# Block 0's output products six steps late, and output weights combined from stored parts

## The chip, the cores and the metric

The kernel runs on one core of a Trainium2 chip. The core has five engines that matter here: TensorE (PE, the matmuls), VectorE (DVE), ScalarE (ACT), GpSimd (POOL) and SyncE (SP, which here only issues transfers). The metric is the device time of one execution in microseconds, as the median of several runs. The kernel before takes 1850.32 us (three runs, 1848.4 to 1851.07).

## The reference

Everything is float32, and the kernel reaches that accuracy by splitting both operands of the large products into a high and a low part.

```python
# attention with keys and values pooled by 8: q, k, v are (8, 8, 576, 64)
k_p, v_p = k.reshape(..., 72, 8, 64).mean(3), v.reshape(..., 72, 8, 64).mean(3)
x = softmax(q @ k_p.T / 8) @ v_p                # to (4608, 512)
# first FFN, d_ff = 2048
h = x @ w_in
g = s * maximum(h, 0)**2 + b
x = g @ w_out
# second FFN, d_ff = 1536
out = (sigmoid(x @ w_gate) * (x @ w_val)) @ w_out2
```

## The kernel before, in words

The 4608 tokens are nine blocks of 512. Attention is done in 18 units of 256 tokens, and the first FFN follows it block by block. Block 0 is computed plainly; blocks 1 to 8 form four pairs, whose output product g @ w_out is done by a scheme of the Strassen kind, with seven products of half-size operands for eight. Its left operands are sums and differences of quarters of w_out, `s1d[x][m]`, which are made once and kept in DRAM; m runs over eight (H1) because w_out's 16 tiles of 128 rows are taken as m and m + 8.

All weights arrive as 64-bit words. `convert` (line 78) makes float32 of a tile in four operations: line 85 on ACT, then lines 86, 87 and 88 on DVE. `split` (line 54) makes a high part on ACT (line 56) and a low part on DVE or POOL (line 57). A product is then three matmuls: high with low, high with high, low with high. `emit_h` (line 259) is one step of the first product, 12 matmuls of 128x512 for 128 of the 2048 columns (lines 269 to 271), followed by relu and square on ACT. `emit_x` (line 411) is the matching output product of block 0, 12 matmuls (lines 419 to 421); `mm_chunk` (line 357) is that of a pair: 6 matmuls for its first three groups of eight chunks and 12 for the last two (lines 370 to 372).

The work from block 0 to the last pair is a list of 176 slots: 16 of block 0, then 40 for each of four pairs. Each slot issues, in this order: the stores that the slot before left behind (`store_later`, line 149, on POOL's queue), the load of the input weights of three steps ahead (`load_wi`, line 129, on SP), a step of the first product, a part of the second FFN's weight preparation (`prep_w2`, line 228), a part of the output weights' combination (`prep_s`, line 178), the conversions of block 0's weights, the splitting of the operands of the output product, attention events for later units, and the output product of two slots before (LAG = 2).

In block 0 each weight tile is converted, split, used and stored (`w1d`, `s1d[0]`, `s1d[1]`, `s1d[3]`). The converted output weights stay in SBUF as `wf[m]`, in the pool of the `gs` tiles, until `prep_s` combines them in slots 14 to 29: six small operations on POOL for each m, then two splits into raw tiles and four stores. The sum `wsum` over all m serves the bias. The raw pool has three tiles of 512 KB and serves the loads of 64-bit weights as well; the pool for input weights has three tiles, the pool for output weights (`wr`) three, the pool for g three.

The order of instructions on PE and SP is the written one from slot 16 on; DVE, ACT and POOL, and all engines before slot 16, are ordered by a scheduler. SP issues in order, so a transfer that waits holds back those behind it.

After slot 175 the second FFN runs over the same pairs. Per m it makes seven products of half-size operands from `w7d[m]` (lines 882 to 884); its gated result goes through `emit_o` (line 929, matmuls in lines 938 to 940) in two phases, the second of which has the weights `wo2d[m]` loaded again. `fetch_w7` and `fetch_wo` are on SP. The operands of its first pair are made by `gen_x` (line 750) in the last pair of the first FFN.

Of the kernel before, what the change touches and what calls it, by code (L numbers as in the profile page):

```python
# [10 lines left out]
I32 = mybir.dt.int32  # L11
# [8 lines left out]
def pooled_attention_two_ffn(ctx, tc, q, k, v, v_left, w_in, w_out, s_in, b_in, w_gate, w_val, w_out2, out):  # L20
# [42 lines left out]
    s1d = [[dram.tile([128, 2, 256], F32, name=f"s1d{x}_{m}") for m in range(H1)] for x in range(7)]  # L63
# [56 lines left out]
    wi_raw, wi, wo_raw, wo, wf = {}, {}, {}, {}, {}  # L120
# [43 lines left out]
    def split_wo(i):  # L164

        if i < M1:
            m = steps[i][1]
            t = wr_tile().rearrange("p (two f) -> p two f", two=2)
            wf[m] = gs_tile()
            split(t[:, 0], t[:, 1], convert(wo_raw.pop(i), wf[m].bitcast(I32)), nc.gpsimd)  # L170
            wo[i] = t
            if m < H1:
                later.append((s1d[0][m], t[:, :, 0:256]))
            else:
                later.append((s1d[1][m - H1], t[:, :, 0:256]))
                later.append((s1d[3][m - H1], t[:, :, 256:512]))

    def prep_s(m, part):

        a, c = wf[m], wf[m + H1]  # L180
# [23 lines left out]
    def prep_bias():  # L204

        bb = cv_tile().bitcast(F32)[:, 0:128]
# [9 lines left out]

    prep = {}
# [41 lines left out]
    def emit_h(i):  # L259
# [12 lines left out]
        if j and m < H1:  # L272
# [138 lines left out]
    def emit_x(i):  # L411
# [10 lines left out]
        if i == M1 - 1:  # L422
            for d, a in enumerate(acc.pop(0)):
# [5 lines left out]
                nc.sync.dma_start(out=x2d[0][:, d, :], in_=eo)  # L429
# [64 lines left out]
    def pool_v_pe(b, what):  # L494

        n = NP if what == "v" else 2
        ps = ps_b.tile([128, n, D], F32, tag="b", name="vps")
# [17 lines left out]
    def place_left(b):  # L515
# [4 lines left out]
        lm = ls if b else at1.tile([128, 2, D], F32, tag="suml", name="lm")  # L520
# [123 lines left out]
    for b in range(1, B):  # L644
# [4 lines left out]
        at(max(p - 13, 0), load_kv, b, "v")  # L649
        at(max(p - 9, 1), pool_v, b, "v", nc.gpsimd)  # L650
# [28 lines left out]
    with tc.manual_schedule():  # L679
# [20 lines left out]
        load_wo(0)  # L700
# [17 lines left out]
        load_wo(1)  # L718
# [8 lines left out]
    if True:  # L727
        values(1, 0)
        values(1, 1)
        split_wo(0)  # L730
# [57 lines left out]

        chunks = [(None, i) for i in range(M1)] + [(p, x) for p in range(NB1) for x in range(5 * H1)]
        hidden, used = {}, []  # L790
        for slot, (p, x) in enumerate(chunks):
            if p is None:
                hidden[slot] = x
            elif x < 4 * H1:
                hidden[slot if p == 0 or x > 1 else slot - H1] = M1 * (1 + 2 * p) + x
            if p is None or x >= 3 * H1 or x % 2:
                used.append((slot + LAG, p, x))
        asked = M1
        light = [slot for slot, (p, x) in enumerate(chunks) if slot >= 2 * M1 + 2 and x < 4 * H1 and (x < 3 * H1 or x % 4 or p != 1)]
        parts = dict(zip(light, (divmod(i, 9) for i in range(9 * M2))))  # L800
        assert len(parts) == 9 * M2, len(parts)

        def mm(slot):
            p, x = chunks[slot]
            if p is None:
                emit_x(x)
            else:
                mm_chunk(p, x)

        pe_order = ExitStack()  # L810
        for slot, (p, x) in enumerate(chunks):
# [4 lines left out]
            store_later()  # L816
# [6 lines left out]
            if slot in parts:  # L823
                prep_w2(*parts[slot])
            if M1 - 2 <= slot < 2 * M1 - 2:
# [210 lines left out]
```

## Time and profile before

| | us |
|---|---|
| median of three runs | 1850.32 |
| profiled execution, device time | 1855.36 |
| profiled execution, span of the trace | 1853.6 |
| PE busy in the span | 1728.0 (93%) |
| DVE busy | 1085.4 (59%) |
| ACT busy | 747.6 (40%) |
| POOL busy | 522.5 (28%) |

The busy share is an average over stages that differ: attention with block 0 up to about 205 us, block 1 to about 306, the remaining pairs to about 1020, then the second FFN. A matmul's busy time overlaps with the next one's, so PE's share is not the share of its peak. Waits are put down to the event that came last.

### The profile page before, as it was taken

To read this page: it belongs to the slowest core of one execution; us is meant where nothing else is said; L and a number is where in the kernel's file an instruction comes from. 1 tells how busy PE (TensorE), PEld (TensorE's weight loads), DVE (VectorE), ACT (ScalarE), POOL (GpSimd) and SP (SyncE) were. 2 spreads that over 40 slices of the span, in tenths; PEclk is the share of its full clock that TensorE was granted. 3 is DMA by queue.
4 is the path that set the end of the run, shared out by engine and by line. 5 is a ranking of instruction groups with operands and counts; after the bars stand their busy time and mean duration, and the time that the engine had idled before them with its cause. 6 is when DMAs were issued, how large, how long until landed. Compare 5 with 4: busy or idle time off the path is not lost.

```text
span 1853.6 us, 22031 instructions
## 1 busy us (share of the span) xinstructions
PE 1728.0 (93%) x7848; PEld 1425.2 (77%) x7848; DVE 1085.4 (59%) x1636; ACT 747.6 (40%) x1331; POOL 522.5 (28%) x615
## 2 busy tenths in 40 slices
PE   4677899999999899989997999999999999999999
PEld 4556688877877777878785888788878887888887
DVE  7999675767675757665486445454445444544111
ACT  2555555646654555546563322222222222222111
POOL 5767961345640645324350000100010001000100
PEclk7788999999999999999998999999999999999999
DMA  7665796888977888878977555755665467555675
GB/s 260 213 210 198 274 332 226 276 298 294 360 247 262 304 306 300 280 248 285 313 266 258 206 203 211 257 188 187 223 249 190 181 221 253 194 180 201 236 238 178
DMA packets 138044, 454.44 MB, mean 245 GB/s; under 512 B 15696, under 2 KB 16720, under 8 KB 137936
## 3 DMA queue, kind: packets, MB, share of 16 engines
q1 hardware_dynamic: 107664, 363.90, 56.4%
q0 software_dynamic: 21056, 72.37, 11.0%
q10 hardware_dynamic: 9216, 16.78, 2.4%
q8 instruction: 62, 1.02, 0.2%
q14 instruction: 46, 0.38, 0.1%
HBM read 371.20 MB, written 81.79 MB: 244 GB/s over the span
## 4 chain that ended last, share of the span: by engine, by line
PE 44%; DMA 3%; POOL 1%; DVE 1%; issue 1%; ACT 0%; SPq 0%; POOLq 0%
PE pc L884 5%; PE pc L882 5%; PE pc L883 5%; PE acc L938 5%; PE acc L940 5%; PE acc L939 5%; PE pb L882 4%; PE pb L884 4%; PE pb L883 4%; DMA wo<-wo2d 2%; POOL raw L57 1%; DMA w<-w7d 1%; DMA g<-b21d 0%; DMA raw<-in 0%; DVE gs L296 0%
## 5 line engine op out<-in xcount | busy, mean ns | idle before, releaser
L888 DVE TENSOR_TENSOR wk<-pc,wk 128x512 f32<-128x512 f32 x192 | 132.4, 690 | 240.7 <-PE pc L884 240.6
L269 PE MATMUL hps<-xl,wi 128*128 128x512 f32 (+1 forms) x584 | 233.4, 400 | 10.9 <-ACT wi L56 7.7
L271 PE MATMUL hps<-xh,wi 128*128 128x512 f32 (+1 forms) x584 | 229.0, 393 | 0.4 <-POOL wi L57 0.4
L270 PE MATMUL hps<-xh,wi 128*128 128x512 f32 (+1 forms) x584 | 229.0, 392 | 0.0
L948 POOL DMA_DIRECT2D out<-eo x32 | 17.3, 543 | 691.0 <-ACT eo L946 685.4
L370 PE MATMUL acc<-gl,wr 128*128 128x512 f32 x448 | 182.5, 407 | 28.7 <-DVE gl L57 19.9
L372 PE MATMUL acc<-gh,wr 128*128 128x512 f32 x448 | 177.2, 396 | 0.0
L371 PE MATMUL acc<-gh,wr 128*128 128x512 f32 x448 | 177.2, 395 | 0.0
L899 ACT ACTIVATE g<-pb 128x512 f32<-128x512 f32 x60 | 35.9, 599 | 345.6 <-PE pb L884 345.6
L884 PE MATMUL pc<-xo,w 128*128 128x512 f32 x432 | 168.1, 389 | 0.0
L883 PE MATMUL pc<-xo,w 128*128 128x512 f32 x432 | 168.1, 389 | 0.0
L882 PE MATMUL pc<-xo,w 128*128 128x512 f32 x432 | 168.0, 389 | 0.0
L57 POOL TENSOR_TENSOR raw<-cv,raw 128x512 fp32r<-128x512 f32 (+1 forms) x72 | 99.3, 1385 | 225.5 <-ACT raw L56 222.3
L57 DVE TENSOR_TENSOR gl<-gs,gh 128x512 fp32r<-128x512 f32 x160 | 129.4, 822 | 34.6 <-ACT gh L56 32.2
L56 ACT ACTIVATE gh<-g 128x512 fp32r<-128x512 f32 x140 | 87.8, 627 | 150.4 <-DVE g L900 141.7
L56 ACT ACTIVATE gh<-gs 128x512 fp32r<-128x512 f32 x160 | 97.3, 627 | 109.3 <-DVE gs L296 106.2
L57 DVE TENSOR_TENSOR gl<-g,gh 128x512 fp32r<-128x512 f32 x140 | 113.6, 812 | 45.7 <-ACT gh L56 40.7
L269 PEld LDWEIGHTS hps<-xl,wi 128*128 128x128 f32 x584 | 112.9, 193 | 34.3 <-ACT wi L56 8.8
L882 PE MATMUL pb<-xo,w 128*128 128x512 f32 x336 | 131.4, 391 | 2.1 <-DMA w<-w7d 2.1
L883 PE MATMUL pb<-xo,w 128*128 128x512 f32 x336 | 131.5, 391 | 0.0
L884 PE MATMUL pb<-xo,w 128*128 128x512 f32 x336 | 131.4, 391 | 0.0
L271 PEld LDWEIGHTS hps<-xh,wi 128*128 128x128 f32 x584 | 111.6, 191 | 24.3 <-POOL wi L57 0.8
(145 smaller groups left out, 3843.2 us busy)
## 6 DMA issues: line engine op xcount, KB each, us to landing
w<-w7d SPq DMA_DIRECT2D x48, 1792.0 KB, 7.7
wi<-w1d SPq DMA_DIRECT2D x128, 512.0 KB, 4.6
wr<-s1d SPq DMA_DIRECT2D x224, 256.0 KB, 4.6
wo<-wo2d SPq DMA_DIRECT2D x108, 512.0 KB, 8.2
raw<-in SPq DMA_DIRECT2D x68, 512.0 KB, 4.8
w7d<-raw POOLq DMA_DIRECT2D x36, 512.0 KB, 5.6
w<-w7d SPq DMA_DIRECT2D x12, 1280.0 KB, 6.9
kv<-in SPq DMA_DIRECT2D x24, 512.0 KB, 6.1
```

Source lines behind the costliest of these rows:

```text
L56: nc.scalar.activation(out=hi, in_=src, func=ACTF.Copy)
L57: eng.tensor_tensor(out=lo, in0=src, in1=hi.bitcast(F32), op=ALU.subtract)
L269: nc.tensor.matmul(out=ps[:, f], lhsT=hi[:, kk], rhs=c[:, kk, f], start=kk == 0, stop=False)
L270: nc.tensor.matmul(out=ps[:, f], lhsT=hi[:, kk], rhs=a[:, kk, f], start=False, stop=False)
L271: nc.tensor.matmul(out=ps[:, f], lhsT=lo[:, kk], rhs=a[:, kk, f], start=False, stop=kk == KD - 1)
L370: nc.tensor.matmul(out=a, lhsT=w[:, 0, f], rhs=gl, start=begin, stop=False, skip_group_check=True)
L371: nc.tensor.matmul(out=a, lhsT=w[:, 0, f], rhs=gh, start=False, stop=False, skip_group_check=True)
L372: nc.tensor.matmul(out=a, lhsT=w[:, 1, f], rhs=gh, start=False, stop=end, skip_group_check=True)
L882: nc.tensor.matmul(out=ps, lhsT=w[:, 0, x, kk], rhs=r[:, 1, kk, :n], start=first and kk == 0, stop=False, skip_group_check=True)
L883: nc.tensor.matmul(out=ps, lhsT=w[:, 0, x, kk], rhs=r[:, 0, kk, :n], start=False, stop=False, skip_group_check=True)
L884: nc.tensor.matmul(out=ps, lhsT=w[:, 1, x, kk], rhs=r[:, 0, kk, :n], start=False, stop=kk == 1, skip_group_check=True)
L888: nc.vector.tensor_tensor(out=o, in0=ps, in1=b_, op=ALU.add)
```

## The change

Block 0's output products stand six steps behind its first products instead of two, and g of block 0 is kept in the `gs` pool. The conversion of w_out comes four slots later (slots 4 to 19), its loads in slots 2 to 17. Pair 0's first eight chunks are made two a slot (operands in slots 21 to 24, products in 22 to 25).

The output weights are combined in slots 16 to 31, from the stored parts: `s1d` gets an eighth part, every m reloads four quarters from DRAM into two raw tiles (a new line 186), DVE adds high and low part (line 191), POOL does four operations on 256 columns and one on 512 for `wsum`, whose halves are added once at the end.

Stores of slots 0 to 19 are issued on SP's queue instead of POOL's, and the four stores of block 0's result on ACT's instead of SP's. The values of batch 1 are pooled by matmuls on PE instead of additions on POOL. The second FFN's weights take eight parts for an m instead of nine (both first loads in one part), not in a pair's twelve-matmul chunks 24 to 31 except in the first pair, and two parts a slot in the last pair from its chunk 13 on. In the second FFN a fetch of the next pair's weights comes after the ninth product of the second phase instead of the fifth.

```diff
-    s1d = [[dram.tile([128, 2, 256], F32, name=f"s1d{x}_{m}") for m in range(H1)] for x in range(7)]
+    s1d = [[dram.tile([128, 2, 256], F32, name=f"s1d{x}_{m}") for m in range(H1)] for x in range(8)]
...
-    def store_later():
+    def store_later(early=False):
         while later:
             dst, t = later.pop(0)
-            nc.gpsimd.dma_start(out=dst, in_=t if t.dtype == F32 else t.bitcast(F32))
+            (nc.sync if early else nc.gpsimd).dma_start(out=dst, in_=t if t.dtype == F32 else t.bitcast(F32))
...
-            wf[m] = gs_tile()
-            split(t[:, 0], t[:, 1], convert(wo_raw.pop(i), wf[m].bitcast(I32)), nc.gpsimd)
+            split(t[:, 0], t[:, 1], convert(wo_raw.pop(i), cv_tile()), nc.gpsimd)
             wo[i] = t
-            if m < H1:
-                later.append((s1d[0][m], t[:, :, 0:256]))
-            else:
-                later.append((s1d[1][m - H1], t[:, :, 0:256]))
-                later.append((s1d[3][m - H1], t[:, :, 256:512]))
+            for h, x in enumerate((0, 7) if m < H1 else (1, 3)):
+                later.append((s1d[x][m % H1], t[:, :, 256 * h:256 * h + 256]))
...
         if part == 0:
+            prep["s"] = []
+            for xs in ((0, 7), (1, 3)):
+                t = raw_tile().bitcast(F32).rearrange("p (two f) -> p two f", two=2)
+                for h, x in zip((h0, h1), xs):
+                    nc.sync.dma_start(out=t[:, :, h], in_=s1d[x][m])
+                prep["s"].append(t)
+        else:
+            a, c = (t[:, 1] for t in prep["s"])
+            for t in prep["s"]:
+                nc.vector.tensor_tensor(out=t[:, 1], in0=t[:, 0], in1=t[:, 1], op=ALU.add)
             tt(c[:, h1], a[:, h1], c[:, h1], ALU.add)
-            if m == 0:
-                tt(wsum[:, h0], a[:, h0], c[:, h0], ALU.add)
-                nc.gpsimd.tensor_copy(out=wsum[:, h1], in_=c[:, h1])
-            else:
-                tt(wsum[:, h0], wsum[:, h0], a[:, h0], ALU.add)
-                tt(wsum, wsum, c, ALU.add)
             tt(a[:, h1], a[:, h0], a[:, h1], ALU.subtract)
             tt(a[:, h0], c[:, h1], a[:, h0], ALU.subtract)
             tt(c[:, h0], c[:, h0], a[:, h0], ALU.subtract)
-        else:
-            for src, xs in ((wf.pop(m), (4, 5)), (wf.pop(m + H1), (6, 2))):
-                t = raw_tile().rearrange("p (two f) -> p two f", two=2)
-                split(t[:, 0].bitcast(F32R), t[:, 1].bitcast(F32R), src, nc.vector)
+            if m == 0:
+                nc.gpsimd.tensor_copy(out=wsum, in_=c)
+            else:
+                tt(wsum, wsum, c, ALU.add)
+            for t, xs in zip(prep["s"], ((4, 5), (6, 2))):
+                split(t[:, 0].bitcast(F32R), t[:, 1].bitcast(F32R), t[:, 1], nc.vector)
                 for x, h in zip(xs, (h0, h1)):
                     later.append((s1d[x][m], t[:, :, h]))
...
-                nc.sync.dma_start(out=x2d[0][:, d, :], in_=eo)
+                nc.scalar.dma_start(out=x2d[0][:, d, :], in_=eo)
...
+        if b == 1:
+            at(0, load_kv, b, "l")
+            at(2, pool_v_pe, b, "v")
+            at(2, place_v, b)
+            at(3, pool_v_pe, b, "l")
+            at(3, place_left, b)
+            continue
...
             if p is None:
                 hidden[slot] = x
+                ready, turn_ = slot + 5, slot + 6
+            else:
+                if x < 4 * H1:
+                    hidden[slot if p == 0 or x > 1 else slot - H1] = M1 * (1 + 2 * p) + x
+                ready, turn_ = slot, slot + LAG
+                if p == 0 and x < H1:
+                    ready, turn_ = M1 + 5 + x // 2, M1 + 6 + x // 2
...
+            if p is not None and slot > 2 * M1:
+                places += [slot] * (1 + (p == NB1 - 1 and x > 12) if x < 3 * H1 else p == 0 and x < 4 * H1)
+        for y, slot in enumerate(places[:8 * M2]):
+            m, r = divmod(y, 8)
+            parts.setdefault(slot, []).extend([(m, 0), (m, 1)] if r == 0 else [(m, r + 1)])
...
-            store_later()
+            store_later(slot < M1 + 4)
...
-            if M1 - 2 <= slot < 2 * M1 - 2:
-                prep_s(*divmod(slot - M1 + 2, 2))
+            if M1 <= slot < 2 * M1:
+                prep_s(*divmod(slot - M1, 2))
...
-                split_g(i)
-                split_wo(i + 1)
-                load_wo(i + 2)
...
+            if 4 <= slot < M1 + 4:
+                split_wo(slot - 4)
+            if 2 <= slot < M1 + 2:
+                load_wo(slot - 2)
...
-                if m == 4:
+                if m == 8:
                     fetch_w7(p, M2 + 1)
```

How the instructions stand now is seen best in three places. The first is DVE where the last weights of block 0 are converted (lines 86 to 88 are a conversion) and the output weights' combination begins. Before:

```order
L575 RECIPROCAL sm<-sm 128x8
L563 TENSOR_TENSOR e<-sps,mx 128x288
L57 TENSOR_TENSOR raw<-gs,raw 128x512
L87 SCALAR_TENSOR_TENSOR gs<-gs,raw 128x512
L57 TENSOR_TENSOR gl<-g,gh 128x512
L57 TENSOR_TENSOR raw<-gs,raw 128x512
L573 TENSOR_REDUCE sm<-e 128x8
L88 SCALAR_TENSOR_TENSOR gs<-raw,gs 128x512
L574 TENSOR_SCALAR sm<-sm 128x8
L575 RECIPROCAL sm<-sm 128x8
```

And with the change, from the second add of the first m to its two splits:

```order
L191 TENSOR_TENSOR raw<-raw 128x512
L562 TENSOR_REDUCE mx<-sps 128x4
L563 TENSOR_TENSOR e<-sps,mx 128x288
L86 TENSOR_SCALAR raw<-raw 128x512
L563 TENSOR_TENSOR e<-sps,mx 128x288
L87 SCALAR_TENSOR_TENSOR cv<-cv,raw 128x512
L88 SCALAR_TENSOR_TENSOR cv<-raw,cv 128x512
L573 TENSOR_REDUCE sm<-e 128x8
L574 TENSOR_SCALAR sm<-sm 128x8
L57 TENSOR_TENSOR raw<-raw 128x512
L575 RECIPROCAL sm<-sm 128x8
L57 TENSOR_TENSOR raw<-raw 128x512
```

The conversion whose line 88 stands in the first piece is the 32nd and last, at DVE's 217th instruction; in the second it is the 31st, at the 240th, and the first m's splits (line 57 on raw) follow it and the adds of line 191.

The second place is SP's queue at the beginning of block 1 (`wi` are input weights of a step, `wr` output weights, `s1d_1_80` and the like the stored parts with m in the middle of the name, `qT` and `kv` loads of attention, `x2d` block 0's result). Both pieces begin with the input weights that slot 17 loads. Before:

```order
L137 DMA wi<-w1d_147 128x1024
L429 DMA x2d_183<-eo 128x512 x4
L307 DMA wr<-s1d_4_83 128x512
L307 DMA wr<-s1d_5_84 128x512
L137 DMA wi<-w1d_148 128x1024
L452 DMA kv<-in 128x1152 x2
L137 DMA wi<-w1d_149 128x1024
L544 DMA qT<-in 128x1024
L307 DMA wr<-s1d_6_85 128x512
L307 DMA wr<-s1d_7_86 128x512
L137 DMA wi<-w1d_150 128x1024
```

And with the change:

```order
L137 DMA wi<-w1d_155 128x1024
L72 DMA raw<-in 128x1024
L152 DMA s1d_0_111<-raw 256x1x256
L152 DMA s1d_0_119<-raw 256x1x256
L152 DMA s1d_0_127<-raw 256x1x256
L152 DMA s1d_0_95<-raw 256x1x256
L152 DMA s1d_6_93<-wr 256x1x256
L152 DMA s1d_6_109<-wr 256x1x256
L137 DMA wi<-w1d_156 128x1024
L186 DMA raw<-s1d_1_80 128x2x256
L186 DMA raw<-s1d_1_136 128x2x256
L186 DMA raw<-s1d_1_88 128x2x256
```

Between the weights of slot 17 and of slot 18 there were only the stores of block 0's result and two loads; now six stores (line 152) stand there, and behind the weights of slot 18 the reloads of the next m (line 186; a fourth follows the three), which wait for a raw tile.

The third place is SP's queue in the last pair, from the `wi` of chunk 18 on, where the loads of the second FFN's weights (line 72) stand between input weights. Before:

```order
L137 DMA wi<-w1d_145 128x1024
L72 DMA raw<-in 128x1024
L307 DMA wr<-s1d_2_97 128x512
L307 DMA wr<-s1d_3_98 128x512
L137 DMA wi<-w1d_146 128x1024
L137 DMA wi<-w1d_147 128x1024
L307 DMA wr<-s1d_4_99 128x512
L307 DMA wr<-s1d_5_100 128x512
L137 DMA wi<-w1d_148 128x1024
L137 DMA wi<-w1d_149 128x1024
L307 DMA wr<-s1d_6_101 128x512
L307 DMA wr<-s1d_7_102 128x512
```

And with the change:

```order
L137 DMA wi<-w1d_153 128x1024
L72 DMA raw<-in 128x1024 x2
L307 DMA wr<-s1d_2_97 128x512
L307 DMA wr<-s1d_3_98 128x512
L137 DMA wi<-w1d_154 128x1024
L137 DMA wi<-w1d_155 128x1024
L307 DMA wr<-s1d_4_99 128x512
L307 DMA wr<-s1d_5_100 128x512
L137 DMA wi<-w1d_156 128x1024
L72 DMA raw<-in 128x1024
L137 DMA wi<-w1d_157 128x1024
L72 DMA raw<-in 128x1024 x2
```

The same `wi` (third step of that stretch, m = 2) stands first in both. Before, one such load stands in these rows and none follows for four more `wi`; now there are five, twice two of them together, ahead of the input weights of the next step.

## Rows read from the trace of the kernel before

**Rows 1.** Windows: us, busy of engines, TensorE's clock, DMA share, GB/s.

```profile
40.00:180.00 140.00, 101.53 (x428) 82.17 (x428) 135.09 (x163) 73.63 (x133) 101.65 (x109) 0.80 0.60 207
180.00:220.00 40.00, 30.11 (x141) 23.95 (x140) 21.98 (x23) 21.62 (x40) 39.08 (x51) 0.96 0.72 245
220.00:306.00 86.00, 85.75 (x440) 72.24 (x441) 57.45 (x86) 45.88 (x88) 44.13 (x55) 0.98 0.84 296
306.00:845.00 539.00, 512.40 (x2454) 423.16 (x2453) 367.30 (x596) 299.41 (x549) 222.60 (x250) 0.99 0.84 288
845.00:985.00 140.00, 130.35 (x590) 107.31 (x590) 90.86 (x135) 84.16 (x153) 62.62 (x62) 0.97 0.84 286
985.00:1020.00 35.00, 29.29 (x112) 23.17 (x111) 21.82 (x36) 10.60 (x18) 0.00 (x0) 0.89 0.72 251
1360.00:1380.00 20.00, 17.00 (x71) 13.70 (x70) 10.72 (x18) 5.98 (x10) 1.92 (x4) 0.93 0.95 352
1560.00:1580.00 20.00, 18.10 (x73) 14.84 (x74) 9.05 (x14) 5.28 (x10) 2.17 (x4) 0.91 0.35 135
```

**Rows 2.** Waits of PE, whole run: us in total, times, longest.

```profile
PE acc L419 <- DVE gl L57: 16.0, 5, 5.4
...
PE acc L938 <- DMA wo<-wo2d: 8.9, 3, 3.0
...
PE hps L269 <- ACT wi L56: 7.7, 3, 6.2
```

**Rows 3.** Line 269 on PE, 205.6 to 306.0 us; then the timeline there.

```profile
L269 PE MATMUL hps<-xl,wi x72: 389/389/499, 205.4 to 303.4; 128*128 128x512 f32 x72
...
306.13 0.39 PE L269 MATMUL hps<-xl,wi 128*128 128x512 f32 x1
306.36 0.39 PE L270 MATMUL hps<-xh,wi 128*128 128x512 f32 x1
```

**Rows 4.** DVE by line, 40 to 240 us; last, a timeline row.

```profile
L86 DVE TENSOR_SCALAR raw<-raw 128x512 int32<-128x512 int32 x29 | 28.1, 970 | 1.0 <-DMA raw<-in 0.9
L88 DVE SCALAR_TENSOR_TENSOR cv<-raw,cv 128x512 int32<-128x512 int32 x15 | 19.1, 1281 | 0.1
...
L87 DVE SCALAR_TENSOR_TENSOR cv<-cv,raw 128x512 int32<-128x512 int32 x15 | 13.0, 871 | 0.2
...
172.91 0.67 DVE L88 SCALAR_TENSOR_TENSOR gs<-raw,gs 128x512 int32<-128x512 int32 x1
```

**Rows 5.** DMA issues, 205 to 306 us: count, KB, us to landing.

```profile
wi<-w1d SPq DMA_DIRECT2D x19, 512.0 KB, 4.4
wr<-s1d SPq DMA_DIRECT2D x20, 256.0 KB, 4.7
s1d<-raw POOLq DMA_DIRECT2D x18, 256.0 KB, 5.7
```

**Rows 6.** DVE by line and shape, 225 to 306 us.

```profile
L57 DVE TENSOR_TENSOR raw<-gs,raw 128x512 fp32r<-128x512 f32 x6 | 7.6, 1268 | 2.2 <-ACT raw L56 2.2
```

**Rows 7.** POOL by line and shape, 225 to 306 us.

```profile
L152 POOL DMA_DIRECT2D s1d<-raw x14 | 9.8, 733 | 5.9 <-DVE raw L57 3.2 <-DVE lt L591 1.5 <-issue 1.2
L184 POOL TENSOR_TENSOR gs<-gs 128x256 f32<-128x256 f32 x6 | 6.0, 993 | 0.1
```

**Rows 8.** ACT by line and shape, 225 to 306 us.

```profile
L56 ACT ACTIVATE raw<-gs 128x512 fp32r<-128x512 f32 x6 | 3.7, 625 | 0.0
```

**Rows 9.** POOL by line and shape, 845 to 985 us.

```profile
L57 POOL TENSOR_TENSOR raw<-cv,raw 128x512 fp32r<-128x512 f32 x13 | 28.6, 2197 | 63.8 <-ACT raw L56 63.8
```

**Rows 10.** DMA issues, 845 to 985 us.

```profile
raw<-in SPq DMA_DIRECT2D x9, 512.0 KB, 6.9
w7d<-raw POOLq DMA_DIRECT2D x9, 512.0 KB, 4.8
```

**Rows 11.** Timeline of POOL, 945 to 965 us: start, us, idle before.

```profile
949.49 11.80 POOL L57 TENSOR_TENSOR raw<-cv,raw 128x512 fp32r<-128x512 f32 x1 [7.65 <-ACT raw L56]
```

**Rows 12.** Timeline of PE, 976 to 986 us.

```profile
984.50 0.80 PE L370 MATMUL acc<-gl,wr 128*128 128x512 f32 x1 [6.75 <-DVE gl L57]
```

More of the change, by code (lines that the diff above doesn't have):

```diff
@@ L204, in prep_bias @@
     def prep_bias():
+        nc.vector.tensor_tensor(out=wsum[:, 0:256], in0=wsum[:, 0:256], in1=wsum[:, 256:512], op=ALU.add)
         bb = cv_tile().bitcast(F32)[:, 0:128]
@@ L271, in emit_h @@
                 nc.tensor.matmul(out=ps[:, f], lhsT=lo[:, kk], rhs=a[:, kk, f], start=False, stop=kk == KD - 1)
-        if j and m < H1:
+        if j == 0 or m < H1:
             g = gs_tile()
@@ L496, in pool_v_pe @@
         n = NP if what == "v" else 2
-        ps = ps_b.tile([128, n, D], F32, tag="b", name="vps")
+        ps = (ps_c if b else ps_b).tile([128, n, D], F32, tag="c" if b else "b", name="vps")
         f = ps.rearrange("p i d -> p (i d)")
@@ L519, in place_left @@
         lh = at1.tile([128, 2, D], F32R, tag="lh", name="lh")
-        lm = ls if b else at1.tile([128, 2, D], F32, tag="suml", name="lm")
+        lm = ls if b > 1 else at1.tile([128, 2, D], F32, tag="suml", name="lm")
         nc.scalar.activation(out=lh, in_=ls, func=ACTF.Copy)
@@ L789, in pooled_attention_two_ffn @@
         chunks = [(None, i) for i in range(M1)] + [(p, x) for p in range(NB1) for x in range(5 * H1)]
-        hidden, used = {}, []
+        NSLOT = len(chunks)
+        hidden, used, made, done = {}, [], {}, {}
         for slot, (p, x) in enumerate(chunks):
@@ L793, in pooled_attention_two_ffn @@
                 hidden[slot] = x
-            elif x < 4 * H1:
-                hidden[slot if p == 0 or x > 1 else slot - H1] = M1 * (1 + 2 * p) + x
+                ready, turn_ = slot + 5, slot + 6
[5 more added lines that the diff above has]
+                    ready, turn_ = M1 + 5 + x // 2, M1 + 6 + x // 2
+            made.setdefault(ready, []).append((p, x))
+            done.setdefault(turn_, []).append((p, x))
             if p is None or x >= 3 * H1 or x % 2:
-                used.append((slot + LAG, p, x))
+                used.append((turn_, p, x))
         asked = M1
-        light = [slot for slot, (p, x) in enumerate(chunks) if slot >= 2 * M1 + 2 and x < 4 * H1 and (x < 3 * H1 or x % 4 or p != 1)]
-        parts = dict(zip(light, (divmod(i, 9) for i in range(9 * M2))))
-        assert len(parts) == 9 * M2, len(parts)
         def mm(slot):
[L804 to L808, printed above, removed]
+            for p, x in done.get(slot, []):
+                if p is None:
+                    emit_x(x)
+                else:
+                    mm_chunk(p, x)
+        places = []
+        for slot, (p, x) in enumerate(chunks):
+            if p is not None and slot > 2 * M1:
+                places += [slot] * (1 + (p == NB1 - 1 and x > 12) if x < 3 * H1 else p == 0 and x < 4 * H1)
+        parts = {}
+        for y, slot in enumerate(places[:8 * M2]):
+            m, r = divmod(y, 8)
+            parts.setdefault(slot, []).extend([(m, 0), (m, 1)] if r == 0 else [(m, r + 1)])
+        assert len(places) >= 8 * M2, len(places)
         pe_order = ExitStack()
@@ L850, in pooled_attention_two_ffn @@
             if i == NS - M1:
-                assert not any(y < 2 * len(chunks) for y in events), events
+                assert not any(y < 2 * NSLOT for y in events), events
                 at_stack.close()
@@ L855, in pooled_attention_two_ffn @@
                 gen_x(0, (i - NS + M1) // 7)
-        for slot in range(len(chunks) - LAG, len(chunks)):
+        for slot in range(NSLOT, NSLOT + LAG):
             mm(slot)
```

33 lines of the change are left out of this document (18 added, 15 removed).

## The prediction

> **What bounds the kernel now.** I read the busy shares by stage first [rows 1], then the waits of PE over the whole run [rows 2], then in each stage the engine or transfer that those waits name. In the first block (40 to 180 us) PE works 101.5 of 140 us while DVE works 135.1: DVE sets the pace. From 220 us PE works 85.75 of 86, so the work of the four pairs is bound by PE, and what is not PE's own work can only be got back at the places where PE waits. The waits that this change touches are three: the output products of block 0 waiting for DVE's low parts (16.0 us in 5 waits) with the first products waiting for the input weights (7.7 us), and the second phase of the last FFN waiting for its output weights (8.9 us in 3) [rows 2]. The edge between front and steady work is the first step of block 1: 18 steps of 12 matmuls begin from 205.4 us on, and the next one, that of slot 34, begins at 306.13 [rows 3]. Matmuls there follow each other by 0.227 us, so a step takes 2.73 us and a slot with its six output products 4.1. The end of the kernel moves by what moves that 306.13, by what changes near the end of the last pair, and by what changes in the last FFN.
>
> **The front: what it could give.** Block 0's output products now stand six steps behind, which takes their 16.0 us and at most the 7.7 us from PE's row of waits. DVE then is what comes next. A conversion costs it 0.97 + 0.87 + 1.28 = 3.1 us [rows 4], and block 1 could start after 27 of the 32 (the output weights' last five come behind it), so 5 x 3.1 = 15.6 us earlier. From the sum of 39.3 the new pooling on PE takes about 7 (32 records at the pitch of 0.227). Without any new wait block 1 would thus start near 173 and slot 34 near 274: 32 us early.
>
> **The front: the new wait.** The combining of the output weights now starts from stored parts. For each of eight m, SP reloads four quarters of 256 KB into two raw tiles; DVE adds in each; POOL needs three small operations before the first tile can be split; ACT and DVE split it; two stores carry it off. There are three raw tiles, so the second tile of m+1 waits until the stores of m's first tile have landed. On SP these loads stand in written order, and the loads of the input weights for three steps later stand behind them; PE waits for those. A round of this chain is due every two slots, which took 2 x 5.6 us before (100.7 us over 18). Its price from rows of 205 to 306 us: landing of a 256 KB reload 4.7 (as wr<-s1d), DVE add 1.1, three POOL operations at 0.99, ACT 0.6, DVE split 1.1, two store issues at 0.73, landing of the store 5.7 [rows 5 to 8]: 17.7 us. For DVE's two operations the rows give 1.27 beside POOL [rows 6] and as little as 0.67 in the last row of [rows 4]; I take a value between. The first m is ready late as well: its splits are DVE's 245th instruction, 28 behind the 217 that before had done when its last conversion ended at 173.6 [rows 4]; at 135.09 / 163 = 0.83 us each [rows 1] that is 173 + 23, say 195. Six further rounds: 195 + 6 x 17.7 = 301, and behind the last reload the weights of slot 34 take 0.7 for the issue and 4.4 to land [rows 5, 7]: 306. The gain of 32 us is used up and the front comes out at 0. Bounds: with every operation at its undisturbed price and one landing hidden the round is 15.5 (-13 us); a round of 12 or less would not be felt at all (-32); at 22, with SP held also by the stores and loads ahead in its queue, +26.
>
> **Stores on SP.** The stores of slots 0 to 19 leave POOL, some 50 at 0.73 us of POOL's time [rows 7], and now sit in SP's ordered queue, where each waits for the split that makes its tile and holds the loads behind it. In the first block POOL had 38 us to spare in 140 [rows 1], so POOL's gain alone is worth nothing to PE; the cost, if any, is inside the bounds above. The Trainium skill (DMA: Bandwidth & Descriptors, "Issuing engines are not separate DMA queues") says that transfers started by any engine share the same 16 DMA engines, so starting them elsewhere saves only the issue time; by it the term is those issues on an engine that isn't the bound, that is nothing. No run of this kernel shows it yet.
>
> **The middle, 306 to 845 us.** The same PE work, the second FFN's weights in eight parts instead of nine and off the slots that have twelve output matmuls. PE works 512.4 of 539 us there [rows 1]; I take 0, with -4 to +5 for shifted waits. The bias's extra add on DVE, the four result stores of block 0 on ACT's queue and the first eight output products of pair 0 done two a slot are at most 1 us each and lie beside PE's work; they are costed at nothing, and at 3 us where PE should have no other work.
>
> **The last pair.** Because parts may not stand in the twelve-matmul slots, the last three of the twelve m must be done two parts a slot, four slots for an m. Four slots are 4 x 4.2 = 16.8 us. A round of an m, from its loads to the tile coming free, takes at its own pace: landing of a load 6.9 [rows 10], a conversion 3.1, fourteen POOL instructions at 62.62 / 62 = 1.01 us [rows 1], landing of the store 4.8 [rows 10], less some 3.5 where the second tile runs beside the first: 25. Both loads of an m now stand together in SP's queue ahead of the input weights, so twice 25 - 16.8 = 8.2 us late; the weights' lead of three slots, 12.6 us, less the 5.1 of their issue and landing pays 7.5 of the 16.4, and POOL is slowed by DVE while the first operands of the last FFN are made. There one POOL subtraction took 11.80 us [rows 11] against 2.20 in the mean [rows 9], so I count half of it: about +5. That makes 16.4 - 7.5 + 5 = 14 late. Of this the wait of 6.75 us before the last products of the pair (at 984.5) [rows 12] goes away, for its cause, DVE's burst, then lies beside the new wait. With it goes the lower clock behind it, 0.89 over 35 us [rows 1], which is 3.9 us, of which I take 3: +4. Bounds: -13 if the loads never hold SP and the 6.75 goes entirely, +20 if each lateness is paid in full.
>
> On POOL's 11.80 us the Trainium skill (SBUF — State Buffer, "SBUF: two separate sides") says that VectorE and GpSimd share a pair of ports as an exclusive lock, held for a whole instruction, the other fully blocked. The row of 11.80 us agrees with it. By that rule alone POOL would do nothing during the burst, which is the third rival below.
>
> **The last FFN.** Fetching the next operands' weights four products later frees the queue for the output weights: the three waits, 8.9 us [rows 2], go. Behind two of them the granted clock stood at 0.93 and 0.91 over 20 us [rows 1], 1.4 and 1.8 us; I take 2.6 of these back: -11.5. At most all, -12; at least -9, since the fetch that now comes behind the ninth product can be late itself and cost some 2.
>
> **Sum.** 0 + 0 + 4 - 11.5 = -7.5. The profiled execution took 1855.4 us, its span 1853.6; it becomes 1847.9. The median of the runs is 5.0 below that execution, so 1843.
>
> **The rivals.** *The chain of reloads isn't felt* (round of 12 us or less, because the reloads run ahead and two landings lie beside each other): -32 + 4 - 11.5 = -39.5, 1811 us. For it: DVE is free from 180 us on (22 of 40 us busy) [rows 1]. Against: the two landings of a round alone are 10.4 us, and POOL was busy 39 of those 40. Chance 0.15. *The chain of reloads is longer than 19 us*, and the kernel is slower: at 22 us a round, because SP has loads, stores and reloads in one order and every one waits for the one before, the front costs +26, less 7.5: 1869 us. From 19 us a round on it undoes all that the other parts give. For it: DMA is busy 0.84 in the stage [rows 1] and the first reload has to wait for parts that are split late. Against: a POOL with fewer stores. Chance 0.25. *POOL is shut out during the burst in the last pair*: a second subtraction of the next m meets it and takes 11.80 us like the one in [rows 11], because two parts a slot put it there. The last pair is then +16 instead of +4, the sum +4.5, the time 1855, hardly slower than now. For it: the 13 subtractions of 845 to 985 us take 2.20 in the mean [rows 9], well over the 0.99 of a half-wide operation in the steady work [rows 7]. Against: only one of them met the burst. Chance 0.15. The forecast holds the rest, 0.45.
>
> **How the numbers follow.** The likeliest case has its own range of 1829 (front at 15.5 us a round) to 1856. To leave out no more than 2 in 10 the range takes in the first rival nearly and the slow one: 1811 to 1869. 0.2% (3.7 us) is what a measurement of this kernel can tell. Faster: 0.15 of the first rival, 0.34 of the forecast's 0.45, 0.03 of the third: 0.52. Same: 0.05 of the third and 0.07 of the forecast: 0.12. Slower: 0.25 of the second, 0.07 of the third, 0.04 of the forecast: 0.36.
>
> **What would show it.** In the profile after: the first step of block 1 near 173 and not 205; then gaps of PE on the input weights every second slot until 306, with SP waiting for the stores of the raw tiles; the step of slot 34 within 13 us of 306; no wait of PE for wo2d in the last FFN; in the last pair a wait on the input weights near the 18th to 26th steps in place of the 6.75. The forecast is wrong if block 1 starts later than 185 (DVE wasn't the bound that I take it for), if PE works through 180 to 300 without a gap, or if SP's waits there come from anything but the raw tiles.

## The result and the profile after

The changed kernel takes 1877.61 us in the median (four runs, 1877.16 to 1879.38), the one before 1850.69 beside it. The ratio is 1.0142, with a 95% interval of 1.0117 to 1.0167: 27 us slower, and 9 us over the upper end of the forecast. The profiled executions, 1877.16 against 1855.36 us with spans of 1875.3 and 1853.6, differ by 22.

To see where the time went, the table follows PE's work through both traces: the first matmul of a step, or the end of a stage, in us from the start of the span.

| point in PE's work | before | after | difference |
|---|---|---|---|
| first step of block 1 (slot 16) | 205.6 | 160.7 | -44.9 |
| step of slot 34 | 306.1 | 311.5 | +5.4 |
| step of the last pair's chunk 21 | 917.3 | 926.4 | +9.1 |
| step of the last pair's chunk 26 | 941.8 | 983.3 | +41.4 |
| last output product of the last pair | 1016.5 | 1050.9 | +34.4 |
| last matmul | 1849.4 | 1871.3 | +21.8 |

So the front ends 5 us late although it began 45 early, the last pair loses 25, and the last FFN gives 12.6 back. The windows of after (columns as in [rows 1]):

```profile
40.00:180.00 140.00, 123.57 (x589) 101.60 (x588) 116.96 (x181) 92.63 (x168) 73.47 (x62) 0.90 0.77 264
220.00:284.00 64.00, 44.93 (x202) 36.27 (x201) 34.35 (x58) 24.84 (x48) 36.59 (x45) 0.86 0.86 296
284.00:312.00 28.00, 14.46 (x53) 11.45 (x53) 7.12 (x12) 6.67 (x12) 13.63 (x17) 0.66 0.64 221
845.00:985.00 140.00, 103.45 (x466) 84.18 (x465) 72.91 (x105) 72.29 (x131) 61.19 (x75) 0.89 0.74 264
```

In the first block PE now works 123.6 of 140 us (101.5 in [rows 1]). From 220 to 312 us, where PE had no gap before, its work and its granted clock both fall (0.86 and 0.66), and once more in the last pair. The waits of PE over the whole run (columns as in [rows 2]):

```profile
PE hps L269 <- DMA wi<-w1d: 44.8, 7, 25.8
...
PE bps L212 <- DVE wsum L207: 13.5, 1, 13.5
...
PE acc L370 <- DMA wr<-s1d: 10.4, 6, 6.8
...
PE acc L419 <- DVE gl L57: 0.6, 1, 0.6
```

Block 0's output products hardly wait any more (0.6 us for 16.0), and no wait for wo2d stands among them. In their place are 44.8 us for input weights, 13.5 us of the bias's matmuls for `wsum`, and 10.4 us for output weights.

**The front.** The first step of block 1 on PE, then DVE's splits of the first m:

```profile
160.66 0.49 PE L269 MATMUL hps<-xl,wi 128*128 128x512 f32 x1
```

```profile
178.62 0.68 DVE L57 TENSOR_TENSOR raw<-raw 128x512 fp32r<-128x512 f32 x1
...
179.33 1.66 DVE L57 TENSOR_TENSOR raw<-raw 128x512 fp32r<-128x512 f32 x1
```

The lead at 160.66 is not all gain: PE still owes six output products of block 0 of 2.7 us each, where before it owed two at its first step of block 1. The first m is split by 181, not by 195. From there the chain of reloads sets the pace; POOL's rows show the first and the last round of eight, and the sum `wsum` of the last:

```profile
174.09 3.92 POOL L179 TENSOR_TENSOR raw<-raw 128x256 f32<-128x256 f32 x4 [4.96 <-DVE raw L191]
...
296.36 3.13 POOL L179 TENSOR_TENSOR raw<-raw 128x256 f32<-128x256 f32 x4 [5.93 <-DVE raw L191]
299.57 1.77 POOL L179 TENSOR_TENSOR wsum<-wsum,raw 128x512 f32<-128x512 f32 x1
```

(296.36 - 174.09) / 7 = 17.47 us a round in the mean; the seven rounds take from 13.7 to 21.8. What PE waits for at the end of it:

```profile
302.54 2.05 PE L212 MATMUL bps<-cv,wsum 128*128 128x128 f32 x8 [13.54 <-DVE wsum L207]
...
311.54 0.39 PE L269 MATMUL hps<-xl,wi 128*128 128x512 f32 x1
```

In slot 32 PE has the bias's matmuls, which need `wsum` of all eight m; it stands 13.54 us, and the step of slot 34 starts at 311.54. The input weights of that step had been there for long; SP issued them behind the last reload (its row, then what the view of that transfer says of its landing):

```profile
292.55 0.54 SPq L137 DMA_DIRECT2D wi<-w1d  x1
```

```profile
DMA to landing us min/median/max: 6.7/6.7/6.7
```

They landed at 299.3, 12.3 us before PE began the step.

**The last pair.** SP's longest wait there, then its timeline, with DVE, ACT, POOL and PE beside it:

```profile
SPq L72 <- DMA w7d<-raw: 49.1, 4, 32.2
```

```profile
937.25 0.85 SPq L137 DMA_DIRECT2D wi<-w1d  x2
...
941.82 0.32 SPq L137 DMA_DIRECT2D wi<-w1d  x1
974.44 0.33 SPq L72 DMA_DIRECT2D raw<-in  x1
974.87 0.40 SPq L137 DMA_DIRECT2D wi<-w1d  x1
```

```profile
941.20 0.43 DVE L86 TENSOR_SCALAR raw<-raw 128x512 int32<-128x512 int32 x1 [0.64 <-DMA raw<-in]
...
949.11 0.69 DVE L57 TENSOR_TENSOR xo<-cv,xo 128x512 fp32r<-128x512 f32 x1 [3.91 <-ACT xo L56]
...
961.24 0.68 DVE L87 SCALAR_TENSOR_TENSOR cv<-cv,raw 128x512 int32<-128x512 int32 x1
...
963.65 0.68 DVE L88 SCALAR_TENSOR_TENSOR cv<-raw,cv 128x512 int32<-128x512 int32 x1
```

```profile
948.45 0.63 ACT L56 ACTIVATE xo<-cv 128x512 fp32r<-128x512 f32 x1 [3.97 <-DMA cv<-x2d]
...
959.51 0.67 ACT L85 ACTIVATE cv<-raw 128x512 f32<-128x512 f32 x1
```

```profile
964.48 0.72 POOL L245 TENSOR_TENSOR cv<-cv 128x256 f32<-128x256 f32 x1 [11.85 <-DVE cv L88]
...
967.94 1.35 POOL L57 TENSOR_TENSOR raw<-cv,raw 128x512 fp32r<-128x512 f32 x1
...
971.05 0.79 POOL L152 DMA_DIRECT2D w7d<-raw  x1
```

```profile
983.27 0.77 PE L269 MATMUL hps<-xl,wi 128*128 128x512 f32 x1 [25.81 <-DMA wi<-w1d]
```

Read backwards: PE waits 25.81 us for input weights that SP issued at 974.87. Ahead of them on SP stands one load, the last output-weight tile of the second FFN (974.44), which waited 32.2 us for a raw tile to be stored. POOL issued that store at 971.05 (it landed at 974.3); before its subtractions POOL had been idle 11.85 us waiting for a conversion. Line 86 of that conversion ran at 941.20 on DVE, line 85 only at 959.51 on ACT, and lines 87 and 88, which need it, at 961.24 and 963.65. On both engines the operands of the last FFN (`xo`) came first, on ACT from 948.45 and on DVE from 949.11 on, and the first of these had itself waited for its load.

### The profile page after: what moved, and what is told of

Read it like the earlier page. It is cut to its first block, busy times and chain, and to the rows that moved or that the text cites. A ratio compares the mean times of both kernels' runs of the same rounds, so it can differ in the third digit from the quotient of the medians.

```text
span 1875.3 us, 22252 instructions
## 1 busy us (share of the span) xinstructions
PE 1732.0 (92%) x7880; PEld 1428.1 (76%) x7880; DVE 1073.2 (57%) x1653; ACT 751.1 (40%) x1331; POOL 473.6 (25%) x558
## 4 chain that ended last, share of the span: by engine, by line
PE 71%; DMA 12%; DVE 11%; POOL 2%; ACT 2%; issue 2%; SPq 1%; ACTq 0%; POOLq 0%; DVEq 0%
PE acc L967 5%; PE pc L912 5%; PE acc L969 5%; PE acc L968 5%; PE pc L913 5%; PE pc L911 5%; PE hps L269 4%; PE hps L271 4%; PE hps L270 4%; PE pb L911 4%; PE pb L912 4%; PE pb L913 4%; DMA raw<-in 4%; PE acc L370 3%; PE acc L371 3%; PE acc L372 3%
## 5 line engine op out<-in xcount | busy, mean ns | idle before, releaser
L269 PE MATMUL hps<-xl,wi 128*128 128x512 f32 (+1 forms) x584 | 237.9, 407 | 51.8 <-DMA wi<-w1d 44.8
L271 PE MATMUL hps<-xh,wi 128*128 128x512 f32 (+1 forms) x584 | 232.3, 398 | 1.1 <-POOL wi L57 1.1
L270 PE MATMUL hps<-xh,wi 128*128 128x512 f32 (+1 forms) x584 | 232.1, 397 | 0.0
L370 PE MATMUL acc<-gl,wr 128*128 128x512 f32 x448 | 183.0, 409 | 17.7 <-DMA wr<-s1d 10.4
L57 DVE TENSOR_TENSOR gl<-gs,gh 128x512 fp32r<-128x512 f32 x176 | 149.5, 862 | 37.1 <-ACT gh L56 34.3
L57 POOL TENSOR_TENSOR raw<-cv,raw 128x512 fp32r<-128x512 f32 (+1 forms) x72 | 89.8, 1253 | 295.9 <-ACT raw L56 149.5
L56 ACT ACTIVATE gh<-gs 128x512 fp32r<-128x512 f32 x176 | 107.3, 627 | 114.0 <-DVE gs L296 98.7
L56 ACT ACTIVATE gh<-g 128x512 fp32r<-128x512 f32 x124 | 77.8, 628 | 154.2 <-DVE g L929 141.7
L271 PEld LDWEIGHTS hps<-xh,wi 128*128 128x128 f32 x584 | 113.6, 195 | 25.8 <-POOL wi L57 1.6
L57 DVE TENSOR_TENSOR gl<-g,gh 128x512 fp32r<-128x512 f32 x124 | 106.5, 859 | 44.7 <-ACT gh L56 40.1
```

Of the source, the lines that this page charges most:

```text
L56: nc.scalar.activation(out=hi, in_=src, func=ACTF.Copy)
L57: eng.tensor_tensor(out=lo, in0=src, in1=hi.bitcast(F32), op=ALU.subtract)
L269: nc.tensor.matmul(out=ps[:, f], lhsT=hi[:, kk], rhs=c[:, kk, f], start=kk == 0, stop=False)
L270: nc.tensor.matmul(out=ps[:, f], lhsT=hi[:, kk], rhs=a[:, kk, f], start=False, stop=False)
L271: nc.tensor.matmul(out=ps[:, f], lhsT=lo[:, kk], rhs=a[:, kk, f], start=False, stop=kk == KD - 1)
L370: nc.tensor.matmul(out=a, lhsT=w[:, 0, f], rhs=gl, start=begin, stop=False, skip_group_check=True)
```

## The experiments

Ratios are against the kernel before on the same chip beside it, whose median lay between 1852.4 and 1854.9 us. The columns on the right are points of PE's work as in the table above.

| run | ratio [95%] | median us | slot 16 | slot 34 | chunk 21 | pair's end | last matmul |
|---|---|---|---|---|---|---|---|
| e1_fetch8 | 0.9924 [0.9898, 0.9950] | 1840.68 | 206.5 | 308.1 | 919.4 | 1017.1 | 1837.4 |
| e2_w2_as_before | 0.9962 [0.9941, 0.9983] | 1845.33 | 161.4 | 311.9 | 923.5 | 1020.1 | 1844.2 |
| e3_bias_late | 1.0109 [1.0072, 1.0147] | 1875.69 | 157.1 | 301.1 | 922.2 | 1048.4 | 1868.8 |
| e4_o_late | 1.0042 [1.0023, 1.0060] | 1860.54 | 159.2 | 312.3 | 935.2 | 1035.3 | 1856.3 |
| e5_bias_w2 | 0.9934 [0.9917, 0.9951] | 1843.18 | 156.8 | 302.6 | 917.1 | 1013.5 | 1837.6 |
| e6_raw4 | 0.9889 [0.9854, 0.9923] | 1834.67 | 160.0 | 287.5 | 898.5 | 989.4 | 1827.8 |
| e7_stores_pool | 1.0021 [0.9999, 1.0043] | 1857.44 | 170.1 | 321.4 | 934.1 | 1029.7 | 1850.7 |
| e8_raw4_pad | 0.9828 [0.9809, 0.9848] | 1824.19 | 160.5 | 287.7 | 896.8 | 990.4 | 1818.0 |
| e9_nopad | 1.0004 [0.9990, 1.0018] | 1855.98 | 157.2 | 302.8 | 918.5 | 1014.3 | 1852.6 |

**e1_fetch8: one part of the change alone, on the kernel before.**

```diff
-                if m == 4:
+                if m == 8:
                     fetch_w7(p, M2 + 1)
```

> The kernel before with one edit: the next pair's weights in the last FFN are fetched after the ninth product of the second phase, not after the fifth. Theory: this part alone gives what the changed kernel shows in the last FFN, where 34.4 us late at its start become 21.7 at the end: 12.7 us faster, so about 1838, and the three waits for wo2d are gone. Rival: the gain there came from a DMA that was quieter because of other parts of the change; then this edit alone gives at most the 8.9 us of the waits, or less if the later fetch is waited for.

Measured 0.9924, 14 us with an interval of 9 to 19; in the trace the last FFN takes 820.3 us (1017.1 to 1837.4) against 832.9 before, 12.6 less, which is what after shows. The windows in which the waits stood (columns as in [rows 1]):

```profile
1360.00:1380.00 20.00, 20.00 (x90) 16.55 (x89) 12.91 (x20) 8.03 (x14) 2.18 (x4) 1.00 0.91 325
1560.00:1580.00 20.00, 20.00 (x90) 16.57 (x89) 10.83 (x17) 4.95 (x9) 1.22 (x3) 1.00 0.48 171
```

PE is busy all 20 us of each and the clock is back at 1.00 (0.93 and 0.91 in [rows 1]). The part works alone, so the rival falls.

**e2_w2_as_before: the change without its order of the second FFN's weights.**

```diff
-        places = []
...
+        light = [slot for slot, (p, x) in enumerate(chunks) if slot >= 2 * M1 + 2 and x < 4 * H1 and (x < 3 * H1 or x % 4 or p != 1)]
+        parts = {slot: [divmod(y, 9)] for y, slot in enumerate(light[:9 * M2])}
```

> The changed kernel with the second FFN's weights prepared in nine parts, one a slot, where they stood before. Theory: the 24 us lost in the last pair come from two parts a slot, whose loads wait in SP's queue for a raw tile ahead of the input weights; the 25.8 us wait goes and the time falls by 20 to 26 us, to 1852 to 1858. Rival: the last pair is slow because VectorE and GpSimd are crowded by the operands of the last FFN at that place, which stay where they are; then 10 us or more of the wait remain and the time is 1865 or more.

Measured 1845.33, a ratio lower by 0.018 than that of after: 33 us. PE's waits from 860 to 1030 us:

```profile
PE acc L370 <- DVE gl L57: 12.2, 5, 7.1
```

No wait for input weights is left there, and the last pair (chunk 21 to its end) takes 96.6 us for 124.5. The 33 us are more than the theory's 20 to 26, and the rival falls; the profiled executions (1850.09 and 1877.16) differ by 27, of which the pair's 27.9 is all.

**e4_o_late: one load moved.** Tells SP's order apart from crowded engines.

```diff
+        for todo in parts.values():
+            if (M2 - 1, 8) in todo:
+                todo.remove((M2 - 1, 8))
+        parts[NSLOT - 12], parts[NSLOT - 11] = [(M2 - 1, 9)], [(M2 - 1, 8)]
...
-            prep["o"] = load64(w_out2[m])
+            if m < M2 - 1:
+                prep["o"] = load64(w_out2[m])
+        elif part == 9:
+            prep["o"] = load64(w_out2[m])
```

> The changed kernel with one load moved: the last output-weight tile of the second FFN is loaded and converted in the last pair's chunks 28 and 29, behind all input weights, instead of 22 and 23. Theory (order of SP's queue): the 25.8 us wait of PE is for input weights that stood behind this one load, so it goes, 20 to 26 us, to 1852 to 1858. Rival (GpSimd and VectorE crowded): the weights are late for other reasons or the pair waits elsewhere; less than 10 us come back.

Measured 1860.54, 18 us under after by the ratios, a little short of the 20 to 26. PE's waits from 860 to 1030 us, then SP's:

```profile
PE hps L272 <- DMA wi<-w1d: 6.1, 2, 5.4
PE acc L373 <- DVE gl L57: 6.1, 3, 2.9
```

```profile
SPq L72 <- DMA w7d<-raw: 24.9, 4, 11.6
```

The 25.8 us wait is gone (5.4 is the longest left) and chunk 21 to the end of the pair takes 100.1 us for 124.5. The crowding on DVE and POOL, which the rival blames, is still there; the same conversion on DVE in this run, and POOL behind it:

```profile
948.37 0.48 DVE L86 TENSOR_SCALAR raw<-raw 128x512 int32<-128x512 int32 x1
...
969.78 0.69 DVE L87 SCALAR_TENSOR_TENSOR cv<-cv,raw 128x512 int32<-128x512 int32 x1
...
971.59 0.69 DVE L88 SCALAR_TENSOR_TENSOR cv<-raw,cv 128x512 int32<-128x512 int32 x1
```

```profile
972.42 2.26 POOL L245 TENSOR_TENSOR cv<-cv 128x256 f32<-128x256 f32 x1 [11.74 <-DVE cv L88]
```

Line 88 follows line 86 by 23.2 us (22.5 in after) and POOL is idle as long, yet PE no longer waits for it. SP's order is thus the cause of the 25.8. What is missing in the sum was lost earlier: this kernel reaches chunk 21 8.8 us later than after; the gap is 0.8 at slot 34 and 7.2 already at the step at 494 us of before. Why, no run shows. The 3.5 us that are left against e2 go with SP's waits behind loads of the two m before (11.6 us at most), which no run takes apart.

**e3_bias_late: the bias ahead of its first use.**

```diff
-            if slot == 2 * M1:
-                prep_bias()
...
         elif z == 1:
+            if p == 0:
+                prep_bias()
```

> The changed kernel with the bias's four matmuls directly ahead of the first use of the bias, at the end of slot 33 instead of in slot 32. Theory: the 13.5 us in which PE waits there for the sum over all m hold back weights that land near 297 and not 307; the step of slot 34 comes 8 to 10 us earlier, 1868 to 1870 in all. Rival: the input weights behind the last reload are as late as the sum, so the wait only moves to them: within 3 us of 1877.6.

```profile
299.42 2.05 PE L212 MATMUL bps<-cv,wsum 128*128 128x128 f32 x8 [9.25 <-DVE wsum L207]
...
301.12 0.77 PE L269 MATMUL hps<-xl,wi 128*128 128x512 f32 x1
```

The step of slot 34 starts at 301.12, 10.4 us earlier, a little more than the theory's 8 to 10. But the wait isn't gone: directly ahead of that step PE still stands 9.25 us for `wsum`, while the weights of slot 34 had landed at 294.1. Of the 10.4, 3.1 come from a sum that is ready sooner (299.42 for 302.54; block 1 begins 3.6 us earlier in this run), and 7.3 from work of slots 32 and 33 that now stands ahead of the wait and not behind it. The time tells little: the ratio is 0.0033 lower with overlapping intervals, and the median of 1875.69 lies in the rival's band. The lead is down to 4.2 us at chunk 21, and at the end of the pair to 2.5, for the long wait there is as long as in after (PE, whole run):

```profile
PE hps L269 <- DMA wi<-w1d: 42.2, 5, 25.9
```

**e5_bias_w2: both edits.** The diffs of e2 and e3 together.

> The changed kernel with both edits, the bias ahead of its first use and the second FFN's weights in nine parts where they stood before. Theory: the bias's 10 us at slot 34, which the run with the late bias alone lost again in the last pair's wait for input weights, now stay: 10 us below the run with the weights as before, 1834 to 1837, and the step of slot 34 near 301. Rival: the gain is given back wherever the next ordered load stands, and it comes out at 1843 to 1847 like that run.

Slot 34 starts at 302.6, 9.3 us before e2's, although PE still stands 8.0 us for `wsum` ahead of it; chunk 21 comes 6.4 and the last matmul 6.6 before. By the ratios it is 0.0028, about 5 us, and the two intervals overlap. The median of 1843.18 is inside the rival's band, but the kernel before ran 4 us slower beside it than beside the changed kernel. So some 5 to 7 of the expected 10 us stay.

**e6_raw4: four raw tiles.** On e5.

```diff
-    const.tile([128, 56], F32, name="pad")
...
-    rawp = w1_stack.enter_context(tc.tile_pool(name="rawp", bufs=3))
+    rawp = w1_stack.enter_context(tc.tile_pool(name="rawp", bufs=4))
-    gs_p = w1_stack.enter_context(tc.tile_pool(name="gs_p", bufs=17))
+    gs_p = w1_stack.enter_context(tc.tile_pool(name="gs_p", bufs=16))
...
-            swap = p is not None and x == 4 * H1 + 1
+            swap = p is not None and x in (4 * H1, 4 * H1 + 1)
```

> As the run with both edits, with four raw tiles instead of three (paid with one tile of the gs pool and the padding, and the next pair's first step of the first product behind the operands of its slot). Theory: the chain of reloads is a ring of three tiles, 17.4 us a round; with four, two rounds overlap and a round needs 10 to 12 us, which is what PE needs for two slots; the step of slot 34 comes 25 to 45 us earlier than 301 and the kernel takes 1790 to 1812. Rival: the round is bound by GpSimd and the DMA engines (0.95 busy from 180 to 220 us), not by the number of tiles: 15 us a round or more, slot 34 at 285 or later, 1820 or more.

SP's wait for raw tiles from 170 to 310 us in after, then in this run, and PE's waits from 158 to 290 us in this run:

```profile
SPq L186 <- DMA s1d<-raw: 54.1, 6, 11.3
```

```profile
SPq L185 <- DMA s1d<-raw: 28.6, 7, 8.3
```

```profile
PE sps L556 <- DVE xl L56: 7.2, 2, 4.2
PE bps L211 <- DVE wsum L206: 6.8, 1, 6.8
```

PE waits no more for input weights there (12.5 us in after), and slot 34 comes at 287.5, 15.1 us before e5 (the exchange of steps in the diff comes only behind it). The theory's numbers fail and the rival's three hold: the round is 15.2 us (POOL's adds of 172.4 to 278.9), slot 34 comes after 285, and the time is over 1820. The rival's reason holds in part only, for the fourth tile did shorten the round and nearly halve SP's wait. The end of the chain is still PE's longest single wait there, 6.8 us of the bias for `wsum`, beside waits for the attention's operands from DVE. The time of 1834.67 hides a part of the gain, since the last FFN took 838.4 us, 14 more than in e5 (824.1).

**e7_stores_pool: stores back on POOL.** On e5.

```diff
-            store_later(slot < M1 + 4)
+            store_later()
```

> As the run with both edits, with all stores on GpSimd's queue as before. Theory: stores were not what bound the front and the ring of raw tiles decides the end of it, so within 4 us of the run with both edits. Rival 1: on SP the stores hold back loads behind them, so back on GpSimd is 5 us or more faster. Rival 2: GpSimd has no room for 50 issues of 0.7 us and splits come later: first step of block 1 10 us or more later, and 5 us or more slower.

Measured 1.0021 against 0.9934 of e5: 16 us slower (14 by the medians), which is rival 2. POOL from 40 to 180 us in e7, and the window 100 to 160 in e7 and in e5 (columns as in [rows 1]):

```profile
L152 POOL DMA_DIRECT2D s1d<-wr x27 | 19.8, 789 | 0.3 <-POOL wr L57 0.3
...
L152 POOL DMA_DIRECT2D w1d<-wi x15 | 9.9, 682 | 0.0
```

```profile
100.00:160.00 60.00, 51.30 (x237) 42.05 (x238) 49.77 (x79) 39.61 (x75) 39.19 (x44) 0.89 0.73 248
```

```profile
100.00:160.00 60.00, 56.56 (x280) 46.55 (x279) 54.87 (x86) 44.56 (x80) 24.89 (x20) 0.97 0.85 286
```

42 stores take 29.7 us of POOL, PE does 51.3 for 56.6 us of work, the first step of block 1 comes 13.3 us later and slot 34 18.8. (DVE's and POOL's order is the scheduler's, and differs between the two kernels in more than the stores.)

**e8_raw4_pad and e9_nopad: where the tiles lie.** e8 is e6 with the padding ahead of the last FFN's tiles, e9 is e5 without the padding.

```diff
+        ctx.enter_context(tc.tile_pool(name="padp", bufs=1)).tile([128, 56], F32, name="pad")
         w7p = ctx.enter_context(tc.tile_pool(name="w7p", bufs=2, reuse_waits="tile"))
```

> As the run with four raw tiles, with the 224 bytes of padding that it dropped put back ahead of the last FFN's tiles. That run's last FFN has its first products at a pitch of 0.2332 us at a granted clock of 1.00, against 0.2267 in the run with three tiles, 4.1 us for each of four pairs. Theory: the pitch comes from where the last FFN's tiles lie in SBUF, so it goes back to 0.2267 and the time falls by 14 to 17 us, to 1817 to 1821. Rival: that run's chip or execution was slower there, or the address that matters is another; then within 4 us of 1834.7.

> As the run with both edits and three raw tiles, without the 224 bytes of padding: the same instructions, tiles 224 bytes lower. Theory (addresses): the last FFN's products go at 0.2332 us and each pair takes 4 us more, 12 to 17 us in all, about 1857. Rival: nothing changes, within 3 us of 1843.

The last FFN's products from 1250 to 1400 us in e5, e9, e6 and e8 (line, shape and count, then busy us and mean ns of one):

```profile
L904 PE MATMUL pc<-xo,w 128*128 128x512 f32 x76 | 29.6, 389 | 0.0
```

```profile
L904 PE MATMUL pc<-xo,w 128*128 128x512 f32 x75 | 29.7, 396 | 0.0
```

```profile
L903 PE MATMUL pc<-xo,w 128*128 128x512 f32 x76 | 30.1, 396 | 0.0
```

```profile
L904 PE MATMUL pc<-xo,w 128*128 128x512 f32 x76 | 29.6, 389 | 0.0
```

With the padding 389 ns, without it 396. From start to start the products' mean is 0.2267 and 0.2332 us. By the ratios e9 takes 13 us more than e5, inside the theory's 12 to 17, and e8 11 us less than e6, a little under its 14 to 17; both rivals fall. What e8 lacks shows in its output products: those on `gh` and `gl` take 395 to 396 ns, against 389 in e5 and 389 to 392 in e6. e8 is the best version: 0.9828 of before, 1824.19 us.

## Why the prediction was wrong

The forecast was "faster", 1843 us. Its sum was 0 (front) + 0 (middle) + 4 (last pair) - 11.5 (last FFN); the profile gives +5.4, +3.7, +25.3 and -12.6.

- **The last pair is the step that failed**, and it lies outside its own bounds (-13 to +20). The prediction had the place, a wait for input weights near the 18th to 26th steps, and the 6.75 us wait that goes away; what it had wrong is the price. I took the lateness of a round of weights, 8.2 us twice, and paid 7.5 of it from the weights' lead: 14 late with POOL's share, where PE waited 32.3 us for input weights. The cost was not that lateness but the longest single wait in SP's queue: one load behind a tile whose conversion ACT and DVE did behind the last FFN's operands, 32.2 us, and all input weights behind it. e4 moves that load and the 25.8 us wait is gone, with the conversion as late as it was; e2 moves the whole order back and the pair is as it was before.
- **The third rival**, POOL shut out during DVE's burst, gave the wrong reason. From 949 to 964 us POOL had one load to issue (0.55 us) and otherwise waited for the conversion; its operations behind the burst take 0.7 to 1.4 us, none like the 11.80 of [rows 11]. The rule of the Trainium skill on the shared ports (SBUF — State Buffer, "SBUF: two separate sides") has nothing to act on there, and e4 shows that order was enough.
- **The round of the reloads was sized right in its mean**: 17.7 predicted, 17.47 measured. A part of that is luck: the stores of the raw tiles landed in 3.3 us in the median where I took 5.7, while POOL's sum for `wsum` (1.8 us), which stands ahead of those stores, isn't in my price. The first m came 14 us earlier than the 195 I took, with DVE's instructions of the first block at 116.96 / 181 = 0.65 us each, not 0.83. By my own sum the weights of slot 34 would then have landed at 292; they did at 299.3, 7 us before my 306, since the last reload was issued at 291.8 and not 287, and the weights behind it took 6.7 us to land and not 4.4.
- **The bias was costed at nothing, 3 us where PE should have no other work; that was the second step that failed.** I counted its extra add, not that its four matmuls stand in PE's order in slot 32 and need the chain's end: 13.5 us. With the weights there at 299.3, the step began at 311.5, 12.3 us later: 7 early and 12.3 late make the +5.4 of the front, so that 0 was nearly met by two errors that worked against each other. e3 takes 10.4 back at slot 34, and even there PE still waits 9.25 for the sum.
- **Stores on SP were costed at nothing and are worth 16 us** (e7). POOL's 38 spare us of 140 were an average over a stage that DVE bound, and the stage after the change is another one. Which of POOL's instructions PE then waits for, and whether the time of issuing is all of it, the runs don't single out. The Trainium skill's sentence that another issuer saves only the issue time (DMA: Bandwidth & Descriptors, "Issuing engines are not separate DMA queues") isn't contradicted: the issues took 0.7 us for each of 42 stores, 29.7 us of POOL in all, more than the 16. The zero was mine, for taking POOL's time to be free.
- **The slow rival** had the sign and, with 1869, nearly the time, but that is luck: it asked for a round of 22 us. The range's upper end rested on it and was 9 us short.
- **The last FFN** was right: -11.5 against -12.6, a little past the bound of -12, and e1 shows it alone.
- **The first rival**, 1811 us with reloads that aren't felt, fell: SP waited 54.1 us for raw tiles from 170 to 310 us. Even e8, with a fourth tile and the two orders mended, reaches slot 34 at 287.7, not near 274, and 1824 us.

What stays open: the attention's work after pair 0's last chunks (up to the step at 437.1 us of before) costs after, e3 and e4 7 to 8 us and the six runs e2 and e5 to e9 at most 1.3. These six have the second FFN's weights in the order of before, so the loss goes with that order; from 424 to 450 us PE waits 8.0 us for operands of the attention in after and 2.1 in e2. Which instruction of the weights is in the way there, no run shows.

## What to carry to other kernels

Where an engine issues in written order, ask of every load that is moved what tile it waits for and who frees that tile; what it costs is that one wait, paid by everything behind it, and not how late its stage is. When a chain is moved later, list every consumer of its last result, small ones on the busiest engine first. A queue that waits for its own stores points to a pool with too few tiles; here one more tile took SP's wait from 54.1 to 28.6 us, but a round only from 17.5 to 15.2, so ask what else stands in the round.

## What the hardware showed that was not expected

The same matmuls on the same instructions ran 3% slower after 224 bytes of padding were dropped: 0.2332 us from start to start in place of 0.2267, at a granted clock of 1.00, in the last FFN's first products, while its output products went at 0.2275 (e9). Restored only ahead of the last FFN's tiles, the padding brought the 0.2267 of the first products back, but then the output products on `gh` and `gl` went slower, 395 to 396 ns for 389 (e8). Which tile's address it is, w7's or another's of that stage, no run here tells.
